# A token-mixing block: the second product over tokens by 2x2 blocks with seven products for eight

## The chip, the cores and the metric

The kernel runs on one core of a Trainium2 chip. A time is the device time of one execution in microseconds; the time of a kernel is the median of its runs. Its engines are TensorE (PE; its weight loads are listed apart as PEld), VectorE (DVE), ScalarE (ACT), GpSimd (POOL) and SyncE (SP), which here issues every DMA. Each engine works through its own queue in order and meets the others at semaphores.

## The reference

One token sequence of S = 2048 tokens with D = 448 channels passes two residual blocks. The second is the one that is changed:

```python
def _B_ref(x, w1, b1, w2, b2):
    h = _layernorm(x, axis=-1)                                  # (B, S, D)
    u = jnp.einsum("bsd,sf->bdf", h, w1) + b1                  # (B, D, F)
    u = _gelu(u)
    y = jnp.einsum("bdf,fs->bds", u, w2) + b2                  # (B, D, S)
    return (lambda x, *d: x.transpose(*d))(y, 0, 2, 1)         # (B, S, D)
...
x = x + ga * _A_ref(h, A_wqkv, A_wo)
h = _layernorm(x, axis=-1) * (1 + cb) + sb
x = x + gb * _B_ref(h, B_w1, B_b1, B_w2, B_b2)
```

The block before it, `_A_ref`, is a linear attention with 16 heads. F is 1792; w1 is 2048 x 1792 and w2 is 1792 x 2048, both in fp32. `mod` rows (`ga`, `cb`, `sb`, `gb` and others) come from a small vector c.

## The kernel before

All of it works on tiles of 128 partitions. Tokens are 16 blocks of 128 (NT), F is 14 blocks of 128 (NF), and the 448 channels are columns. The order of the work is written out by hand: the kernel lists the instructions, and each engine keeps the order of the listing. SBUF tiles come from a pool of 94 slots of 128 x 512 fp32 (`slots`), and a new tile waits until the one that had its slot before is used up. PSUM has 8 banks.

Matmuls of full precision are made of reduced ones. A matrix is split in two F32R tiles, a high part (a rounded copy, ACT) and a low part (the rest, a subtraction on DVE); this is `split`, L52 to L54. A product then takes three matmuls into one PSUM tile: high by high, high by low and low by high (`acc3`, L527 to L530).

The stages are: attention's projections and sums (to about 133 us); attention's output and two layernorms per token block, beside the first four blocks of the first product (to about 240 us); the rest of the first product, u = gelu(h w1), and the second one, y = u w2.

Both products over tokens go through one loop (L624 to L644). w1 and w2 come in pieces of 128 rows and up to 512 columns (`W1G`, `W2G`, `pieces`), loaded 8 steps ahead (`load_to`) and split 3 steps ahead (`split_to`). A step is one piece: for each of its up to four blocks of 128 columns, the three matmuls of `acc3`, with 448 columns of h or u as the moving operand. Each group of blocks has its own PSUM banks, so that the results of the group before are taken out while the next group runs: `finish_u` (L606) makes gelu, the product with gb and the split of one u block, `finish_y` (L614) adds x and stores one block of the output. The residual x waits in 16 slots, and gb * b2 is added to it in the first 16 steps (L640). w2 has six groups, the last two of one block each.

Of the kernel before, what the change touches and what calls it, by code (L numbers as in the profile page):

```python
# [33 lines left out]
def block_kernel(ctx: ExitStack, tc: tile.TileContext, x, wqkv, wo, w1, b1, w2, b2, c, wmod, out):  # L34
    nc = tc.nc
    xf = x.flatten_outer_dims()
    of = out.flatten_outer_dims()

    slots = ctx.enter_context(tc.tile_pool(name="slots", bufs=94))
    small = ctx.enter_context(tc.tile_pool(name="small", bufs=4))  # L40
    cst = ctx.enter_context(tc.tile_pool(name="cst", bufs=1))
    psum = ctx.enter_context(tc.tile_pool(name="psum", bufs=8, space=bass.MemoryType.PSUM))

    ctx.enter_context(tc.manual_schedule())

    def slot(name, w=D, dt=F32, parts=P):
        return slots.tile([parts, w], dt, name=name, tag="slot", padded_shape=[P, 512])

    def bank(name):
        return psum.tile([P, 512], F32, name=name, tag="bank")  # L50

    def split(full, hi, lo):  # L52
        nc.scalar.activation(hi, full, AF.Copy)  # L53
        nc.vector.tensor_sub(lo, full, hi.bitcast(F32))  # L54

# [12 lines left out]
    mhalf = cst.tile([P, 2], F32, name="mhalf")  # L68
    nc.vector.memset(mhalf, -0.5)

# [33 lines left out]
    load_qkv(0)  # L104
    load_x(3)

# [1 line left out]
    warm = bank("warm")  # L108

    def keep_warm(n):  # L110
# [2 lines left out]

    keep_warm(WARM)

# [1 line left out]
    ec = cst.tile([G, 4], F32, name="ec")  # L117
    nc.scalar.activation(ec, c_sb, AF.Exp, scale=-1.0)
    sc = cst.tile([G, 4], F32, name="sc")
# [35 lines left out]
        else:  # L155
            nc.vector.tensor_sub(w[64:128], r[64:128], w[64:128].bitcast(F32))

# [25 lines left out]

# [1 line left out]
    heads, hs, st = {}, {}, {}  # L185

    def a_mean(t):
# [99 lines left out]
    def a_q(t):  # L287
        qps[t] = project(t, 0, "qp")
        del heads[t]
# [61 lines left out]
    for t in range(NT):  # L351
# [42 lines left out]
        if t == 4:  # L394
            for g in range(4):
                w = slot(f"wo{g}", parts=G + 1)
# [3 lines left out]
            b1c = cst.tile([P, NF], F32, name="b1c")  # L400
# [7 lines left out]
            split_to(t + 1 - 16 + PRE)  # L408
    cb1, sb, gb = mods[4], mods[3], mods[5]

# [1 line left out]
    a_q(late.pop(0))  # L412
    load_to(PRE + MID + 3)
    split_to(PRE + MID)
# [10 lines left out]
    nc.scalar.activation(zb, zp[:, :D], AF.Copy)  # L425
    Wph, Wpl = [], []

# [99 lines left out]
    def acc3(ps, hi, lo, sl, mh, ml, first, last):  # L527
        nc.tensor.matmul(ps[:, :D], hi[:, sl], mh, start=first, stop=False)  # L528
        nc.tensor.matmul(ps[:, :D], hi[:, sl], ml, start=False, stop=False)  # L529
        nc.tensor.matmul(ps[:, :D], lo[:, sl], mh, start=False, stop=last)  # L530
# [18 lines left out]
    accs, early = None, []  # L549
    for i in range(NT + LAG):  # L550
# [19 lines left out]
        scale, res, norm1, norm2 = i + 1 < NT, 0 <= i - 2 < NT, 0 <= i - 3 < NT, 0 <= i - 4 < NT  # L570
# [29 lines left out]
        if res or norm1:  # L600
            b_rstd(i, 0 if res else 1, 2 if norm1 else 1)

# [1 line left out]
    Uh, Ul = [None] * NF, [None] * NF  # L604

    def finish_u(f, ps):  # L606
        u = slot(f"u{f}")
        nc.scalar.activation(u, ps[:, :D], AF.Gelu_apprx_tanh, bias=b1c[:, f:f + 1])  # L608
        nc.vector.tensor_mul(u, u, gb)  # L609
        Uh[f] = slot(f"uh{f}", dt=F32R)  # L610
        Ul[f] = slot(f"ul{f}", dt=F32R)
        split(u, Uh[f], Ul[f])

    def finish_y(t, ps):  # L614
        o = slot(f"o{t}")
        nc.vector.tensor_add(o, ps[:, :D], X[t])  # L616
        nc.sync.dma_start(of[t * P:(t + 1) * P, :], o)

    k = NT
    pending = [(finish_u, f, accs[f]) for f in range(4)]  # L620
    xleft = list(range(NT))
    groups = [(w1, f0, n) for f0, n in W1G[1:]] + [(w2, t0, n) for t0, n in W2G]
    k += LAG - 1
    for w, o0, n in groups:  # L624
        up = w is w1
        steps = NT if up else NF
        if early:
            accs, first = early, LAG - 1
            early = None
        else:  # L630
            accs, first = [bank(f"{'up' if up else 'yp'}{o0 + i}") for i in range(n)], 0
        for r in range(first, steps):
            load_to(k + AHEAD)
            split_to(k + 3)
            if pending:
                fn, idx, ps = pending.pop(0)
                fn(idx, ps)
            if xleft:
                t = xleft.pop(0)
                nc.vector.scalar_tensor_tensor(X[t], gb, b2c[:, t:t + 1], X[t], op0=ALU.mult, op1=ALU.add)  # L640
            mh, ml = (H2h[r], H2l[r]) if up else (Uh[r], Ul[r])
            step(k, accs, mh, ml, r == 0, r == steps - 1)
            k += 1
        pending += [(finish_u if up else finish_y, o0 + i, accs[i]) for i in range(n)]  # L644
    for fn, idx, ps in pending:
        fn(idx, ps)


_INS = ['A_x', 'A_wqkv', 'A_wo', 'B_w1', 'B_b1', 'B_w2', 'B_b2', 'c', 'w_mod']
# [23 lines left out]
```

## Time and profile before

| what | value |
|---|---|
| median of 3 runs | 480.47 us (480.19 to 481.48) |
| the profiled execution: span from its first to its last instruction | 476.1 us |
| PE busy | 467.2 us, 98% of the span |
| PEld, DVE, ACT, POOL busy | 425.6, 287.0, 194.2, 26.3 us |
| mean granted TensorE clock | 0.988 |
| first product: first and last matmul start | 159.6 and 335.9 us |
| second product: first and last matmul start | 336.1 and 472.1 us |
| DMA | 45.55 MB, mean 96 GB/s |

The page gives no time for the profiled execution beside its span; the median of the runs is 4.4 us over that span. A group's row has the line of the kernel, the engine, the operation, the tiles that it writes and reads, their shape and number, and then the busy time in us, the mean of one in ns, and the idle time of the engine ahead of them with what ended most of it. A timeline's row has the start and the time from the first to the last end, in us, and the number of instructions that it merges.

### The profile page before, as it was taken

The numbers are of one execution on the slowest core, as the hardware profiler recorded it, in microseconds if no ns is written. First come the engines' busy times: TensorE is split into PE (matmuls) and PEld (weight loads), VectorE is DVE, ScalarE is ACT, GpSimd is POOL, SyncE is SP. The second block draws the span as 40 slices with busy tenths as digits, with TensorE's granted clock in tenths as the row PEclk, the third lists the DMA queues.
The fourth block names the chain that finished last, engine by engine and source line by source line (L and its number), as shares of the span: only waits on it lengthen the run. The fifth ranks groups of instructions, "written<-read, shape, count | busy, mean of one in ns | idle before, by whom it ended". The sixth has DMA issues, their size and how long they took to land.

```text
span 476.1 us, 6824 instructions
## 1 busy us (share of the span) xinstructions
PE 467.2 (98%) x2384; PEld 425.6 (89%) x2384; DVE 287.0 (60%) x672; ACT 194.2 (41%) x419; POOL 26.3 (6%) x62
## 2 busy tenths in 40 slices
PE   6999999999999999999999999999999999999996
PEld 4788899999799999999999999999999999999996
DVE  5789988755888887898538657035620711603243
ACT  1653333335536746666646045034630330500332
POOL 2020211100001010111100000000000000000000
PEclk8799999999999999999999999999999999999999
DMA  8998221005020111112201232018600830801432
GB/s 235 292 274 176 89 67 42 23 23 178 0 67 23 45 44 45 45 45 87 70 1 47 65 111 88 22 53 287 215 0 1 272 115 18 281 0 49 141 115 74
DMA packets 35651, 45.55 MB, mean 96 GB/s; under 512 B 7904, under 2 KB 24096, under 8 KB 35616
## 3 DMA queue, kind: packets, MB, share of 16 engines
q1 hardware_dynamic: 35616, 45.10, 31.5%
q8 instruction: 19, 0.31, 0.3%
q14 instruction: 16, 0.13, 0.1%
HBM read 41.42 MB, written 3.67 MB: 95 GB/s over the span
## 4 chain that ended last, share of the span: by engine, by line
PE 96%; DMA 1%; DVE 1%; SPq 1%; issue 0%; POOL 0%; ACT 0%; DVEq 0%
PE up L530 10%; PE yp L528 10%; PE yp L529 10%; PE up L528 10%; PE yp L530 10%; PE up L529 10%; PE op L477 8%; PE vp L266 8%; PE qp L266 8%; PE kp L266 7%; PE kvb L308 3%; PE tp L247 2%; PE tq L461 1%; DMA wm<-in_w_mod_dram 1%; PE modp L141 1%; PE wp L541 1%
## 5 line engine op out<-in xcount | busy, mean ns | idle before, releaser
L53 ACT ACTIVATE ph<-pr 128x512 fp32r<-128x512 f32 (+2 forms) x148 | 70.1, 518 | 97.3 <-DMA pr<-in_B_w_dram 94.1
L54 DVE TENSOR_TENSOR pl<-pr,ph 128x512 fp32r<-128x512 f32 (+2 forms) x148 | 77.3, 557 | 25.4 <-ACT ph L53 24.5
L530 PE MATMUL up<-h2h,pl 128*128 128x448 f32 x224 | 81.9, 366 | 0.0
L528 PE MATMUL up<-h2h,ph 128*128 128x448 f32 x224 | 81.8, 365 | 0.0
L530 PE MATMUL yp<-uh,pl 128*128 128x448 f32 x224 | 81.8, 365 | 0.0
L528 PE MATMUL yp<-uh,ph 128*128 128x448 f32 x224 | 81.8, 365 | 0.0
L529 PE MATMUL yp<-ul,ph 128*128 128x448 f32 x224 | 81.8, 365 | 0.0
L529 PE MATMUL up<-h2l,ph 128*128 128x448 f32 x224 | 81.8, 365 | 0.0
L616 DVE TENSOR_TENSOR o<-yp,x 128x448 f32<-128x448 f32 x16 | 9.9, 621 | 70.6 <-PE yp L530 70.6
L530 PEld LDWEIGHTS up<-h2h,pl 128*128 128x128 f32 x224 | 42.1, 188 | 3.6 <-DVE pl L54 0.3
L529 PEld LDWEIGHTS up<-h2l,ph 128*128 128x128 f32 x224 | 42.1, 188 | 3.3
L528 PEld LDWEIGHTS up<-h2h,ph 128*128 128x128 f32 x224 | 42.1, 188 | 3.3
L528 PEld LDWEIGHTS yp<-uh,ph 128*128 128x128 f32 x224 | 42.1, 188 | 3.3
L529 PEld LDWEIGHTS yp<-ul,ph 128*128 128x128 f32 x224 | 42.1, 188 | 3.3
L530 PEld LDWEIGHTS yp<-uh,pl 128*128 128x128 f32 x224 | 42.1, 188 | 3.3
L609 DVE TENSOR_TENSOR u<-u,mod 128x448 f32<-128x448 f32 x14 | 8.7, 620 | 40.6 <-ACT u L608 40.6
L608 ACT ACTIVATE u<-up,b1c 128x448 f32<-128x448 f32 x14 | 8.7, 622 | 46.1 <-PE up L530 46.1
L266 PE MATMUL kp<-wh,hh 128*128 128x448 f32 x64 | 24.7, 386 | 0.0
L477 PE MATMUL op<-wph,pth 112*128 112x448 f32 x64 | 24.6, 385 | 0.0
L266 PE MATMUL vp<-wh,hh 128*128 128x448 f32 x64 | 24.6, 384 | 0.0
L266 PE MATMUL qp<-wh,hh 128*128 128x448 f32 x64 | 24.1, 377 | 0.0
L266 PE MATMUL kp<-wh,hl 128*128 128x448 f32 x64 | 23.5, 368 | 0.0
(119 smaller groups left out, 766.2 us busy)
## 6 DMA issues: line engine op xcount, KB each, us to landing
pr<-in_B_w_dram SPq DMA_DIRECT2D x90, 256.0 KB, 3.4
wm<-in_w_mod_dram SPq DMA_DIRECT2D x24, 196.0 KB, 5.7
pr<-in_B_w_dram SPq DMA_DIRECT2D x30, 128.0 KB, 2.4
x<-in_A_x_dram SPq DMA_DIRECT2D x16, 224.0 KB, 4.0
out_dram<-o SPq DMA_DIRECT2D x16, 224.0 KB, 3.1
wr<-in_A_wqkv_dram SPq DMA_DIRECT2D x9, 224.0 KB, 5.3
pr<-in_B_w_dram SPq DMA_DIRECT2D x28, 64.0 KB, 2.0
wo<-in_A_wo_dram SPq DMA_DIRECT2D x4, 196.0 KB, 5.6
```

The source lines that it names most:

```text
L53: nc.scalar.activation(hi, full, AF.Copy)
L54: nc.vector.tensor_sub(lo, full, hi.bitcast(F32))
L247: nc.tensor.transpose(tps[t][:, ch * P:(ch + 1) * P], h[:, ch * P:(ch + 1) * P], ident)
L266: nc.tensor.matmul(o, a[:, s], b, start=(n == 0), stop=(n == 10))
L308: nc.tensor.matmul(kvb[:G + 1, g * G:(g + 1) * G], v[:, g * (G + 1):(g + 1) * (G + 1)], pk[:, g * G:(g + 1) * G], start=(t == 0 and g == 0 ...
L477: nc.tensor.matmul(opb[t][:, :D], a[:, s], b, start=(n == 0), stop=(n == 11))
L528: nc.tensor.matmul(ps[:, :D], hi[:, sl], mh, start=first, stop=False)
L529: nc.tensor.matmul(ps[:, :D], hi[:, sl], ml, start=False, stop=False)
L530: nc.tensor.matmul(ps[:, :D], lo[:, sl], mh, start=False, stop=last)
L608: nc.scalar.activation(u, ps[:, :D], AF.Gelu_apprx_tanh, bias=b1c[:, f:f + 1])
L609: nc.vector.tensor_mul(u, u, gb)
L616: nc.vector.tensor_add(o, ps[:, :D], X[t])
```

## The change

The second product is cut in blocks of 2 x 2: for each pair of token blocks (t0, t1), each pair of f blocks (even and odd), and the two halves of the channels (224 columns each, `HD`). Of such a pair of 2 x 2 matrices the product is formed with seven products of blocks for eight, in the form of Strassen and Winograd. With a11, a12, a21 and a22 for w2's blocks (the first digit of each name goes with the token block, the second with the even or odd f), its sums are s1 = a21 + a22, s2 = s1 - a11, s3 = a11 - a21 and s4 = a12 - s2; u's are t1 to t4, from the halves of an even and an odd u block. The seven products are a11 b11, a12 b21, s2 t2, s1 t1, s3 t3, s4 b22 and a22 t4.

- Each part of u lies in one tile of 448 columns, its high half beside its low half (`u_parts`). A product of two blocks is then two matmuls, the high part of w2 by all 448 columns and the low part by the 224 columns of the high half (`mult2`), and its two column halves are added when it is taken out of PSUM. There are 8 x 7 x 7 = 392 such pairs of matmuls for 672 matmuls of 448 columns.
- w2 is loaded as `a11` to `a22` for all of F and one token block at a time, in tiles of 4 and of 3 blocks, with rows of 512 bytes (`load_quads`). GpSimd makes the sums of w2 (`sums2`, and s4 in `lo2`) and those of u. ACT and DVE split each of the seven operands in high and low parts (`hi2`, `lo2`), two products ahead of PE.
- PSUM tiles are copied (`copy2`) and added to x in place (`out2`, `evac2`), and the output is stored from x.
- x from token block 2 on is written to DRAM in the first product and fetched again a pair at a time (`xpark`, `fetch_x`), and its addition of gb * b2 is made in every second step.
- The first product's third group of four f blocks is cut in two of two.

```diff
-    W1G = [(0, 4), (4, 4), (8, 4), (12, 2)]
-    W2G = [(0, 4), (4, 4), (8, 4), (12, 2), (14, 1), (15, 1)]
+    W1G = [(0, 4), (4, 4), (8, 2), (10, 2), (12, 2)]
     pieces = [(w1, t, f0, n) for f0, n in W1G for t in range(NT)]
-    pieces += [(w2, f, t0, n) for t0, n in W2G for f in range(NF)]
...
+    def u_parts(r, name, src):
+        w = slot(f"u{name}_{r}", dt=F32R)
+        split(src, w[:, :HD], w[:, HD:])
+        uops[name, r] = w
+
+    def finish_u(f, ps):
+        r = f // 2
+
+        def act():
+            u = ufull[f] = slot(f"u{f}")
+            nc.scalar.activation(u, ps[:, :D], AF.Gelu_apprx_tanh, bias=b1c[:, f:f + 1])
+            nc.vector.tensor_mul(u, u, gb)
+            if f % 2 == 0:
+                return
+            u0 = ufull[f - 1]
+            ta, tb = ufull["a", r], ufull["b", r] = slot(f"ta{r}"), slot(f"tb{r}")
+            nc.gpsimd.tensor_tensor(ta[:, :HD], u0[:, HD:], u0[:, :HD], op=ALU.subtract)
+            nc.gpsimd.tensor_tensor(ta[:, HD:], u[:, HD:], ta[:, :HD], op=ALU.subtract)
+            nc.gpsimd.tensor_tensor(tb[:, :HD], u[:, HD:], u0[:, HD:], op=ALU.subtract)
+            nc.gpsimd.tensor_tensor(tb[:, HD:], u[:, :HD], ta[:, HD:], op=ALU.subtract)
+
+        def part(key, half, name):
+            return lambda: u_parts(r, name, ufull[key][:, half * HD:(half + 1) * HD])
+
+        if f % 2 == 0:
+            return [act, part(f, 0, "b11")]
+        two = lambda p, q: lambda: (p(), q())
+        return [act, part(f, 0, "b21"), two(part(("a", r), 1, "t2"), part(("a", r), 0, "t1")),
+                two(part(f, 1, "b22"), part(("b", r), 0, "t3")), part(("b", r), 1, "t4")]
+
+    w2v = w2.rearrange("(r e p) c -> e p r c", e=2, p=P)
...
+    def load_quads(q):
+        for name, (fo, to) in QUADS.items():
+            raw2[q, name] = []
+            for r0, n in RS:
+                w = slot(f"{name}_{q}_{r0}", n * P)
+                c0 = (2 * q + to) * P
+                nc.sync.dma_start(w.rearrange("p (r c) -> p r c", c=P), w2v[fo, :, r0:r0 + n, c0:c0 + P])
+                raw2[q, name].append(w)
+
+    def sub(q, out, a, b, op=ALU.subtract, into=None):
+        res = []
+        for i, (r0, n) in enumerate(RS):
+            w = raw2[q, into][i] if into else slot(f"{out}_{q}_{r0}", n * P)
+            nc.gpsimd.tensor_tensor(w, raw2[q, a][i], raw2[q, b][i], op=op)
+            res.append(w)
+        raw2[q, out] = res
+
+    def sums2(q):
+        sub(q, "s1", "a21", "a22", ALU.add)
+        sub(q, "s2", "s1", "a11")
+        sub(q, "s3", "a11", "a21", into="a21")
+
+    PRODS = (("a11", "b11", 0), ("a12", "b21", 1), ("s2", "t2", 0), ("s1", "t1", 2), ("s3", "t3", 0),
+             ("s4", "b22", 2), ("a22", "t4", 0))
+    todo2 = [(q, m) for q in range(NT // 2) for m in range(7)]
...
+    def hi2(n):
+        while cnt["hi"] < min(n, len(todo2)):
+            q, m = todo2[cnt["hi"]]
+            a = PRODS[m][0]
+            hilo[q, m] = []
+            for w, (r0, nr) in zip(raw2[q, a], RS):
+                h = slot(f"{a}h_{q}_{r0}", nr * P, F32R)
+                nc.scalar.activation(h, w, AF.Copy)
...
+    def lo2(n):
+        while cnt["lo"] < min(n, len(todo2)):
+            q, m = todo2[cnt["lo"]]
+            a = PRODS[m][0]
+            for i, (r0, nr) in enumerate(RS):
+                hl = hilo[q, m][i]
+                hl[1] = slot(f"{a}l_{q}_{r0}", nr * P, F32R)
+                nc.vector.tensor_sub(hl[1], raw2[q, a][i], hl[0].bitcast(F32))
+            cnt["lo"] += 1
+            if a == "a12":
+                sub(q, "s4", "a12", "s2", into="a12")
+
+    def mult2(q, m):
+        a, b, k = PRODS[m]
+        opens = m in (0, 1, 3)
+        if opens:
+            acc2[q, k] = bank(f"y{q}_{k}")
+        ps = acc2[q, k]
+        closes = m in (1, 5, 6)
+        parts2 = hilo.pop((q, m))
+        for r in range(PAIRS):
+            (h, l), i = parts2[r // 4], r % 4
+            w = uops[b, r]
+            s = slice(i * P, (i + 1) * P)
+            nc.tensor.matmul(ps[:, :D], h[:, s], w, start=opens and r == 0, stop=False, skip_group_check=True)
+            nc.tensor.matmul(ps[:, :HD], l[:, s], w[:, :HD], start=False, stop=closes and r == PAIRS - 1,
+                             skip_group_check=True)
+
+    def copy2(q, k, name):
+        cop[q, name] = slot(f"c{name}_{q}")
+        nc.scalar.activation(cop[q, name], acc2[q, k][:, :D], AF.Copy)
+
+    def out2(q, k, name, t, half):
+        c, x = cop.pop((q, name)), X[t][:, half * HD:(half + 1) * HD]
+        nc.vector.tensor_add(c, acc2[q, k][:, :D], c)
+        nc.vector.tensor_add(x, x, c[:, :HD])
+        nc.vector.tensor_add(x, x, c[:, HD:])
...
+    def evac2(q, m):
+        t0, t1 = 2 * q, 2 * q + 1
+        if m == 0:
+            copy2(q, 0, "c1")
+        elif m == 1:
+            out2(q, 1, "c1", t0, 0)
+        elif m == 2:
+            copy2(q, 0, "c2")
+        elif m == 3:
+            copy2(q, 2, "c5")
+        elif m == 4:
+            out2(q, 0, "c5", t1, 1)
+            if q == NT // 2 - 1:
+                store(t1, 1)
+        elif m == 5:
+            out2(q, 2, "c2", t0, 1)
+            store(t0)
+        else:
+            x = X[t1][:, :HD]
+            nc.vector.tensor_add(x, acc2[q, 0][:, :HD], x)
+            nc.vector.tensor_add(x, acc2[q, 0][:, HD:D], x)
+            store(t1, 0 if q == NT // 2 - 1 else None)
...
+    jobs = [j for f in range(4) for j in finish_u(f, accs[f])]
+
+    xleft = list(range(NT))
+    xpark = [park.tile([P, D], F32, name=f"xpark{t}") for t in range(NT)]
+
+    def fetch_x(q):
+        for t in (2 * q, 2 * q + 1):
+            if X[t] is None:
+                X[t] = slot(f"xb{t}")
+                nc.sync.dma_start(X[t], xpark[t])
...
+        for r in range(first, NT):
             load_to(k + AHEAD)
             split_to(k + 3)
+            if jobs:
+                jobs.pop(0)()
+            if xleft and k % 2:
                 t = xleft.pop(0)
                 nc.vector.scalar_tensor_tensor(X[t], gb, b2c[:, t:t + 1], X[t], op0=ALU.mult, op1=ALU.add)
+                if t >= 2:
+                    nc.sync.dma_start(xpark[t], X[t])
+                    X[t] = None
+            step(k, accs, H2h[r], H2l[r], r == 0, r == NT - 1)
             k += 1
+            if k == len(pieces) - 15:
+                load_quads(0)
+            if k == len(pieces) - 12:
+                sums2(0)
+            if len(pieces) - k in (9, 6, 3):
+                hi2(cnt["hi"] + 1)
+                lo2(cnt["lo"] + 1)
+        jobs += [j for i in range(n) for j in finish_u(o0 + i, accs[i])]
+
+    load_quads(1)
+    for i in (0, 2, 1, 3):
+        jobs[i]()
+    jobs = jobs[4:]
+    for n, (q, m) in enumerate(todo2):
+        if m == 0:
+            fetch_x(q)
+        if m == 3 and q + 2 < NT // 2:
+            load_quads(q + 2)
+        hi2(n + 3)
+        lo2(n + 3)
+        if m == 1 and q + 1 < NT // 2:
+            sums2(q + 1)
+        mult2(q, m)
+        if jobs:
+            jobs.pop(0)()
+        evac2(q, m)
...
```

More of the change, by code (lines that the diff above doesn't have):

```diff
@@ L601, in block_kernel @@
             b_rstd(i, 0 if res else 1, 2 if norm1 else 1)
-    Uh, Ul = [None] * NF, [None] * NF
-    def finish_u(f, ps):
[L607 to L617, printed above, removed]
+    HD = D // 2
@@ new lines, in block_kernel @@
+    w2v = w2.rearrange("(r e p) c -> e p r c", e=2, p=P)
+    raw2, comb = {}, {}
+    QUADS = {"a11": (0, 0), "a12": (1, 0), "a21": (0, 1), "a22": (1, 1)}
+    def load_quads(q):
[6 more added lines that the diff above has]
+                raw2[q, name].append(w)
@@ new lines, in block_kernel @@
+    todo2 = [(q, m) for q in range(NT // 2) for m in range(7)]
+    hilo = {}
+    cnt = {"hi": 0, "lo": 0, "quads": 0, "sums": 0}
+    def hi2(n):
[6 more added lines that the diff above has]
+                nc.scalar.activation(h, w, AF.Copy)
+                hilo[q, m].append([h, None])
+            cnt["hi"] += 1
@@ new lines, in copy2, with store @@
+    def copy2(q, k, name):
[6 more added lines that the diff above has]
+        nc.vector.tensor_add(x, x, c[:, HD:])
+    def store(t, half=None):
+        s = slice(0, D) if half is None else slice(half * HD, (half + 1) * HD)
+        nc.sync.dma_start(of[t * P:(t + 1) * P, s], X[t][:, s])
@@ L619, in block_kernel @@
     k = NT
-    pending = [(finish_u, f, accs[f]) for f in range(4)]
+    jobs = [j for f in range(4) for j in finish_u(f, accs[f])]
     xleft = list(range(NT))
-    groups = [(w1, f0, n) for f0, n in W1G[1:]] + [(w2, t0, n) for t0, n in W2G]
+    xpark = [park.tile([P, D], F32, name=f"xpark{t}") for t in range(NT)]
[4 more added lines that the diff above has]
+                nc.sync.dma_start(X[t], xpark[t])
     k += LAG - 1
-    for w, o0, n in groups:
-        up = w is w1
-        steps = NT if up else NF
+    for o0, n in W1G[1:]:
@@ L630, in block_kernel @@
         else:
-            accs, first = [bank(f"{'up' if up else 'yp'}{o0 + i}") for i in range(n)], 0
-        for r in range(first, steps):
+            accs, first = [bank(f"up{o0 + i}") for i in range(n)], 0
+        for r in range(first, NT):
             load_to(k + AHEAD)
             split_to(k + 3)
[L635 to L638, printed above, removed]
+            if jobs:
+                jobs.pop(0)()
+            if xleft and k % 2:
                 t = xleft.pop(0)
                 nc.vector.scalar_tensor_tensor(X[t], gb, b2c[:, t:t + 1], X[t], op0=ALU.mult, op1=ALU.add)
-            mh, ml = (H2h[r], H2l[r]) if up else (Uh[r], Ul[r])
-            step(k, accs, mh, ml, r == 0, r == steps - 1)
+                if t >= 2:
+                    nc.sync.dma_start(xpark[t], X[t])
+                    X[t] = None
+            step(k, accs, H2h[r], H2l[r], r == 0, r == NT - 1)
             k += 1
-        pending += [(finish_u if up else finish_y, o0 + i, accs[i]) for i in range(n)]
-    for fn, idx, ps in pending:
-        fn(idx, ps)
+            if k == len(pieces) - 15:
[23 more added lines that the diff above has]
+        evac2(q, m)
 _INS = ['A_x', 'A_wqkv', 'A_wo', 'B_w1', 'B_b1', 'B_w2', 'B_b2', 'c', 'w_mod']
```

4 lines of the change are left out of this document (added).

## The prediction

> **What bounds the kernel now.** I read the page's first part, then the groups by form, the stage of the second product by a window, and timelines of the spots where one engine holds up another.
>
> ```profile
> span 476.1 us, 6824 instructions
> PE 467.2 (98%) x2384; PEld 425.6 (89%) x2384; DVE 287.0 (60%) x672; ACT 194.2 (41%) x419; POOL 26.3 (6%) x62
> ...
> L530 PE MATMUL yp<-uh,pl 128*128 128x448 f32 x224 | 81.8, 365 | 0.0
> ...
> 335.90:472.40 136.50, 136.50 (x674) 126.18 (x672) 47.43 (x100) 37.51 (x85) 0.00 (x0) 1.00 0.32 104
> ```
>
> The last row is the second product, 335.9 to 472.4 us: PE never stops, the granted clock is 1.00, DVE is busy a third of the time and POOL not at all. 672 matmuls in 136.5 us are 0.203 us each; the 365 ns of a row is latency, since matmuls overlap. So this stage costs matmul starts, and a change pays if it removes starts and nothing else becomes the slowest.
>
> **What a narrower matmul costs.** The new one has 224 columns and no row has that shape with F32R operands. The nearest are at a change from transposes of 128 columns to the projection:
>
> ```profile
> 59.91 0.60 PE L247 MATMUL tp<-ident,h 128*128 128x128 f32 x4
> ...
> 60.23 0.19 PEld L266 LDWEIGHTS vp<-wh,hh 128*128 128x128 f32 x1
> 60.34 0.19 PEld L266 LDWEIGHTS vp<-wl,hh 128*128 128x128 f32 x1
> 60.55 0.19 PEld L266 LDWEIGHTS vp<-wh,hl 128*128 128x128 f32 x1
> ```
>
> Four transposes span 0.60 us with a last one of 0.27, hence 0.11 us from start to start. The F32R weight load at 60.23 is followed by the next after 0.11 us, although each lasts 0.19: loads overlap, and one takes a slot of 0.11. Behind a 448-column matmul the spacing is 0.20 to 0.21. So columns set the 0.203 and the load the 0.11. Half the columns would be 0.203/2 = 0.10, below the load's slot: I take **0.11**. Bounds: 0.109 (the transposes), and 0.203 if the matmul's cost did not fall with its columns.
>
> **The change on PE.** 8 block pairs of tokens x 7 products x 7 pairs of f = 392 pairs of one 448-column and one 224-column matmul, instead of 672 wide ones. 392 x (0.203 + 0.11) = 122.7 us against 136.5: **13.8 us less** if PE stays the bound. One block pair (49 pairs) is then 15.3 us of PE.
>
> **DVE in that stage.** Durations overlap by 0.085 back to back: five pl of 512 columns (686 ns) span 3.09 us, 0.601 each. By the pl rows of 512, 256 and 128 columns (686, 420, 288 ns) and the 621 ns of the 448-column add, less 0.085: 512 is 0.60, 384 is 0.47, 448 is 0.535, 224 is 0.30. Per block pair: the low halves in lo2, 7 x (0.60 + 0.47) = 7.5; the evacuation, 3 x (0.535 + 2 x 0.30) + 2 x 0.30 = 4.0. Sum 11.5 us of 15.3, where before it had 47.4/136.5, one third. ACT: 7 x (0.62 + 0.51) + 3 x 0.54 = 9.5, hidden. The PSUM banks are not reused at once: another product of 2.2 us lies between a copy and the next matmul into its bank.
>
> **POOL in that stage.** It gets s1 to s4 per block pair, 4 x (512 + 384) columns; no such operation is in the trace. Lower bound, the slope of affine_select (677 ns at 448 columns, 292 at 128, so 1.2 ns a column): 0.75 + 0.60, or 5.4 us in all. Upper: POOL's tensor_tensor has a base of 0.41 (0.552 us with one column, 0.691 with two), and two inputs might cost twice the slope: 1.64 + 1.33, 11.9 us. I take base and single slope, 1.02 + 0.87, **7.6 us**, nearer the affine_select, which like the sums has no power in it. [...] Alone, POOL fits too.
>
> **But the two share something.** These rows are, on POOL and DVE, one power that took 0.99 us, and an ordinary one that took 0.55:
>
> ```profile
> 19.18 0.69 DVE L230 SCALAR_TENSOR_TENSOR h<-x,an,mod 128x448 f32<-128x448 f32 x1
> 19.28 0.99 POOL L225 TENSOR_TENSOR rs<-ve,mhalf 128x1 f32<-128x1 f32 x1 [13.28 <-DVE ve L223]
> ...
> 33.84 0.68 DVE L54 TENSOR_TENSOR hl<-tp,hh 128x512 fp32r<-128x512 f32 x1
> 34.07 0.55 POOL L225 TENSOR_TENSOR rs<-ve,mhalf 128x1 f32<-128x1 f32 x1 [4.60 <-DVE ve L223]
> ```
>
> In the first, DVE reads x and mod, both in SBUF, until 19.87, and the power ends 0.40 us after that: it needs whatever DVE holds from 0.14 us after its start. In the second, DVE's tp lies in PSUM, and POOL is not held. Two more powers are stretched the same way (691 ns at 5.3 us, 747 ns at 26.0), and those beside L487, which reads PSUM, are not. So a DVE operation with both inputs in SBUF keeps POOL waiting to its end. All of lo2 and the adds of the copies to x are such: 7.5 + 6 x 0.30 = 9.3 us per block pair. Whether a long POOL operation holds DVE in turn, no row shows.
>
> [...]
>
> If both ways hold, POOL holds 7.6 - 8 x 0.14 = 6.45 us per block pair. DVE plus that is 18.0, or 15.8 if all its 2.2 us on PSUM run under POOL. I take half, 16.9, plus 8 broken overlaps of 0.085: **17.6 us**, over PE's 15.3. DVE's queue then sets the pace, since PE waits for each low half. Before PE can run the last block pair (15.3; POOL has only s4 there), DVE must do 47 of 56 steps of the loop, 6.7 x 17.6 = 117.9, less three low halves made before the stage (3.2), plus the last u pair (0.54 + 7 x 0.30 = 2.6). Stage: 132.6 + 0.3 for the start = 132.9, or **3.6 us less** than 136.5. It breaks even at 18.1 us per block pair.
>
> **The other parts.** At the start of the second product the last u's are late: both gelu, both multiplies and one split lie between the last up matmul and b11 of the last pair, some 2.2 us; it is needed after 6 of 7 steps, 1.9 us. Hence the 0.3; if the chain queued behind the s2 halves it would be 2. The regrouped w1 (two groups of two blocks for one of four) moves no matmul; it adds 16 small loads and splits, and DVE's 0.335 per 256-column split lies in steps of 6 x 0.203 = 1.22 us. The u parts cost DVE 7 x 0.30 instead of 2 x 0.54 per pair, beside PE. POOL's four u sums have 16 steps. Each parked x is a store that waits on SP for its DVE add (L640 before), with the next w1 load queued behind it; loads are 8 steps ahead and splits 3, so 5 steps or 6 us cover a landing of 2.4 to 3.4. Uncovered it would cost about 2 us each. Quads arrive in rows of 512 bytes: the last w2 groups had those too (64 KB, 2.0 us to landing). A block pair moves 1.83 MB of w2, and x in and out, 2.75 MB in 15 us or more, under 185 GB/s, while 289 was reached. fetch_x waits on SP behind the store of the pair before, and DVE needs it about 4.4 us later against a landing of 4.0: covered barely; at worst 1 us per block pair. The tail, two dependent 224-column adds and a half store, is as long as before within 0.2.
>
> **Forecast.** The span is 476.1; the median 480.47 holds 4.4 outside it that I leave. 480.5 - 3.6 = 476.9, less part of a microsecond as POOL often falls into DVE's waits for PE: **476 us**.
>
> **Rivals.**
> - *DVE is never held* (POOL alone waits, in the 15.3 - 9.3 = 6.0 us that DVE leaves, against 6.45): PE keeps the pace, 480.5 - 13.8 + 0.3 + about 1 = 468. For it: no row shows DVE waiting; at 25.47 a power begins and L230 starts 0.18 later with its usual 0.68. [...] 24%.
> - *The two are wholly serial*: no PSUM work falls under POOL, 18.7 us per block pair, stage 6.7 x 18.7 - 0.6 + 15.6 = 140.3, 484 us; at POOL's upper price 22.3 us and 508. It decides from 18.1 on. 22%.
> - *A narrow matmul costs a full slot*: 784 x 0.203 = 159.2, 503 us. It loses from 0.145 on. Against: the loads 0.11 apart. 12%.
> - A late x or a start-up stall adding more than 5 us: 4%.
>
> Forecast itself, 471 to 480: 38%. About 0.3% (1.4 us) is what a measurement can tell from no change. Faster: the 24% and most of the 38%, 0.56; same 0.09; slower 0.35. Range 467 to 492: it leaves out the narrow matmul's 12% and a few per cent of POOL's upper price.
>
> **What would show it.** PE starts in the new stage: 0.203 and 0.11 by pairs where it does not wait. DVE's L693 rows at 686 ns or stretched towards 1.5 us when POOL's L659 runs; L659 itself at about 1.0 and 0.87, or stretched. PE's waits in the stage on DVE's low halves, about 10 us in sum. Wrong would be: L713 spaced like the wide ones, PE without waits, or PE waiting on ACT, DMA or x.

## The result, and the profile after

The changed kernel is slower. Its median is 495.24 us (494.82 to 496.33, 4 runs); the kernel before ran beside it in 480.97 us (4 runs). The ratio is 1.032, with a 95% interval of 1.028 to 1.035. The profiled execution took 494.82 us, with a span of 493.1 us. Every execution of the kernel before that is on record with its span took 1.7 to 1.9 us more than that span. So of the 4.4 us between its median and the span of its profile, some 2.7 are not time outside the span: the profile is of a quicker execution than the median one. On record that kernel took 476.1 to 481.5 us.

These are the span, the busy times and three rows of the forty slices on the page of the changed kernel:

```profile
span 493.1 us, 7571 instructions
PE 464.0 (94%) x2496; PEld 423.4 (86%) x2496; DVE 405.3 (82%) x823; ACT 235.0 (48%) x522; POOL 145.5 (30%) x154
...
PE   6899999999999999999999999979798897897897
DVE  5789988755888878996388598495999999999995
...
POOL 2021110000000110111034242076653954944920
```

PE was full to the end before. Now its row has 7s and 8s in the last third, just where DVE's row goes to 9 and POOL's wakes up. The second product as a window (length; then the busy times of PE, PEld, DVE, ACT and POOL with their instructions; the clock, the DMA share and GB/s), and what PE waited for in the whole execution (total, times, longest):

```profile
341.33:489.26 147.93, 131.48 (x785) 122.80 (x783) 141.81 (x201) 66.90 (x139) 82.56 (x60) 0.95 0.41 123
```

```profile
PE y L713 <- DVE s3l L693: 16.2, 7, 3.6
PE modp L142 <- DVE acc L134: 3.5, 2, 1.9
PE up L529 <- DVE pl L55: 2.9, 2, 2.2
```

DVE, busy a third of this stage before, is now busy 141.81 of 147.93 us. PE stands still seven times, once in every block pair but the last, and each time for the low half of the fifth product (s3l). In the first product it waits twice for a low half of w1 (`pl`), which it did not do before. Why DVE is late is seen in timelines of one block pair, DVE first and POOL after it (start, us, and how many alike in a row):

```profile
399.69 1.15 DVE L693 TENSOR_TENSOR a12l<-a,a12h 128x512 fp32r<-128x512 f32 x2
...
403.76 3.07 DVE L693 TENSOR_TENSOR s1l<-s,s1h 128x512 fp32r<-128x512 f32 x2
406.76 0.61 DVE L722 TENSOR_TENSOR cc<-y,cc 128x448 f32<-128x448 f32 x1
407.40 0.84 DVE L723 TENSOR_TENSOR xb<-xb,cc 128x224 f32<-128x224 f32 x1
408.27 1.07 DVE L724 TENSOR_TENSOR xb<-xb,cc 128x224 f32<-128x224 f32 x1
409.26 3.03 DVE L693 TENSOR_TENSOR s3l<-a,s3h 128x512 fp32r<-128x512 f32 x2
```

```profile
400.51 2.91 POOL L659 TENSOR_TENSOR a<-a,s 128x512 f32<-128x512 f32 x2 [7.14 <-DVE a12l L693]
403.38 3.03 POOL L659 TENSOR_TENSOR s<-a,a 128x512 f32<-128x512 f32 x2
406.38 2.71 POOL L659 TENSOR_TENSOR s<-s,a 128x512 f32<-128x512 f32 x2
409.05 2.82 POOL L659 TENSOR_TENSOR a<-a,a 128x512 f32<-128x512 f32 x2
```

The two halves of a12l (512 and 384 columns), made while POOL rests, take 1.15 us. Those of s1l and s3l, made beside POOL's sums, take 3.07 and 3.03. L723 and L724 are stretched too, from 0.39 to 0.84 and 1.07. L722 between them runs beside a sum as well and keeps its 0.61: one of its inputs, y, lies in PSUM. So in these rows DVE is held by POOL where both its inputs lie in SBUF. POOL is held less: its two sums take 2.9 here, and 1.40 + 1.01 at their fastest.

The 17.0 us by which the span grew (the medians grew by 14.3) are in two places. The second product starts 5.3 us later (336.07 to 341.33), 4.9 of it because the first product is longer. It is itself 11.7 us longer, from its first matmul's start to its last one's end (136.4 to 148.1). The tail differs by less than 0.1.

### The profile page after: what moved, and what is told of

Same layout as the page of the kernel before. It is cut to its first block, busy times and chain, and to the rows that moved or that the text cites. A ratio compares the mean times of both kernels' runs of the same rounds, so it can differ in the third digit from the quotient of the medians.

```text
span 493.1 us, 7571 instructions
## 1 busy us (share of the span) xinstructions
PE 464.0 (94%) x2496; PEld 423.4 (86%) x2496; DVE 405.3 (82%) x823; ACT 235.0 (48%) x522; POOL 145.5 (30%) x154
## 5 line engine op out<-in xcount | busy, mean ns | idle before, releaser
L55 DVE TENSOR_TENSOR pl<-pr,ph 128x256 fp32r<-128x256 f32 (+1 forms) x80 | 46.5, 595 | 10.1 <-ACT ph L54 9.3
L512 POOL TENSOR_TENSOR rt<-vw,mhalf 128x2 f32<-128x2 f32 (+1 forms) x17 | 11.5, 674 | 114.9 <-DVE vw L510 114.9
L718 ACT ACTIVATE cc<-y 128x448 f32<-128x448 f32 x24 | 13.1, 544 | 65.0 <-PE y L713 60.6
L54 ACT ACTIVATE ph<-pr 128x256 fp32r<-128x256 f32 (+1 forms) x80 | 38.3, 492 | 8.9 <-PE up L528 3.9
L659 POOL TENSOR_TENSOR a<-a,s 128x512 f32<-128x512 f32 (+1 forms) x16 | 25.3, 1600 | 56.7 <-DVE a12l L693 56.7
L713 PE MATMUL y<-ut,s3l 128*128 128x224 f32 x56 | 17.4, 311 | 16.2 <-DVE s3l L693 16.2
L713 PEld LDWEIGHTS y<-ut,s3l 128*128 128x128 f32 x56 | 12.4, 221 | 18.4 <-DVE s3l L693 18.2
L626 POOL TENSOR_TENSOR ta<-u 128x224 f32<-128x224 f32 x7 | 10.1, 1437 | 57.8 <-DVE u L621 43.1
L464 ACT ACTIVATE pth<-tq 112x512 fp32r<-112x512 f32 x16 | 9.6, 598 | 33.2 <-PE tq L460 29.4
L265 PE MATMUL kp<-wh,hh 128*128 128x448 f32 x64 | 24.6, 384 | 0.0
L265 PE MATMUL vp<-wh,hh 128*128 128x448 f32 x64 | 24.6, 384 | 0.0
L659 POOL TENSOR_TENSOR s<-a,a 128x512 f32<-128x512 f32 (+1 forms) x16 | 23.7, 1501 | 0.0
```

The costliest lines, as they stand in the source:

```text
L265: nc.tensor.matmul(o, a[:, s], b, start=(n == 0), stop=(n == 10))
L659: nc.gpsimd.tensor_tensor(w, raw2[q, a][i], raw2[q, b][i], op=op)
L713: nc.tensor.matmul(ps[:, :HD], l[:, s], w[:, :HD], start=False, stop=closes and r == PAIRS - 1, skip_group_check=True)
L718: nc.scalar.activation(cop[q, name], acc2[q, k][:, :D], AF.Copy)
```

## The experiments

A time below is a median where several runs were made, and the single run's time otherwise. The kernel before, on the chips of the three sets of runs, had medians of 477.8 (e1 to e4), 478.8 (e5 to e8) and 478.6 us (e9 to e11). "Period" is the time from one block pair's first matmul to the next one's, for a block pair in the middle of the stage. "Stage" is the second product's length as above.

### e1: the sums of w2 on DVE

```diff
-            nc.gpsimd.tensor_tensor(w, raw2[q, a][i], raw2[q, b][i], op=op)
+            nc.vector.tensor_tensor(w, raw2[q, a][i], raw2[q, b][i], op=op)
```

> Edit: the sums of w2 (s1 to s4) on DVE instead of POOL; u's sums stay on POOL. Theory 'port' (a DVE and a POOL operation that both read two SBUF tiles exclude each other): DVE 11.5 + 4 x 1.07 = 15.8 us per block pair against PE's 15.36, nothing is stretched; second product 126 to 132 us instead of 147.9, first product as in the changed kernel, time 473 to 480. Rival 'load' (DVE's own work and its in-order queue, two products ahead, are too much; POOL does not matter): 4.3 us more on DVE per block pair, 18.5 becomes about 22.8, second product about 180, time about 527. Rival 'latency' (POOL's sums are late, DVE waits for them): like 'port', 124 to 130.

477.37 us, ratio 0.998 (0.995 to 1.001): the same time as the kernel before, and 3% less than the changed one. A block pair as a window, and PE's wait:

```profile
372.25:388.92 16.67, 15.63 (x101) 14.66 (x99) 16.43 (x34) 8.37 (x17) 0.00 (x0) 1.00 0.57 166
```

```profile
PE y L713 <- DVE s3l L693: 7.9, 7, 1.8
```

DVE has eight operations more per block pair and is finished earlier: the period falls from a mean of 18.55 us (the second to the seventh block pair) to 16.67. The L693 rows are back at 0.69 and 0.55 us. So the eight sums cost more of DVE's time when POOL makes them than when DVE does. The first product is 177.7 us long instead of 181.2 (176.3 before). The stage takes 134.9 us, more than the 126 to 132 expected by 'port'; 'latency' was given a stage like that of 'port', so this run doesn't tell the two apart.

### e2: no sums of w2

```diff
-        res = []
-        for i, (r0, n) in enumerate(RS):
-            w = raw2[q, into][i] if into else slot(f"{out}_{q}_{r0}", n * P)
-            nc.gpsimd.tensor_tensor(w, raw2[q, a][i], raw2[q, b][i], op=op)
-            res.append(w)
-        raw2[q, out] = res
+        raw2[q, out] = raw2[q, into or a]
```

> Edit: the sums of w2 are left out (the quads themselves are split and multiplied in their place), so POOL is idle in the second product; all splits, matmuls and loads stay. 'Port' and 'latency': PE sets the pace, 8 x 15.36 = 123 us plus under 2 at the start, time about 472. 'Load': second product stays at 147.9, time 495.

464.15 us. This is the second product as a window:

```profile
335.08:458.46 123.38, 123.08 (x785) 117.29 (x783) 100.78 (x201) 65.54 (x139) 3.16 (x4) 1.00 0.49 145
```

PE never stops for more than 0.4 us, the period is 15.35 us, and the first product is back at 176.3. What the changed kernel loses against this, 24.6 us in the second product and 4.9 in the first, hangs on the sums of w2. The time is 8 us under the 472 expected: 4.9 are the first product, where no gain was reckoned with, and the kernel before is 3 us quicker on this chip too.

### e3: POOL only writes

```diff
-            nc.gpsimd.tensor_tensor(w, raw2[q, a][i], raw2[q, b][i], op=op)
+            for _ in range(3):
+                nc.gpsimd.memset(w, 0.5)
```

> Edit: each sum of w2 becomes three memsets of the same tile on POOL: POOL is occupied for about as long (512 columns took 1.40 us, a memset of 448 took 0.47), the tiles and the waits on them stay, the values of the sums are left out. POOL then reads nothing. 'Port' (only reads collide): L693 back at 0.68 and 0.55 us, second product 123 to 127, time about 472 to 476. 'Latency': stalls at s3 as before, 140 to 148, time about 490 to 495. 'Load': 147.9, 495.

464.67 us. One block pair:

```profile
366.90:382.20 15.30, 15.30 (x100) 14.62 (x99) 12.42 (x26) 8.16 (x17) 10.94 (x24) 1.00 0.63 181
```

POOL is as busy as in the changed kernel (10.94 us of a period, 11.4 there), and DVE's rows are not stretched: it needs 12.42 us. So neither the time that POOL is busy nor the waits between the two queues hold DVE, but that POOL reads from SBUF: DVE is busy 12.42 us of a block pair beside writes, and in the changed kernel 18.3 beside reads (the mean of the last two windows of this document). The stage of 123.5 us is the one that 'port' expected; the time is below its 472 to 476, for the same reasons as in e2.

### e4: the sums of u on DVE

The four `nc.gpsimd.tensor_tensor` of `finish_u` become `nc.vector.tensor_tensor`; the sums of w2 stay on POOL.

> Edit: the four sums of each u pair on DVE instead of POOL; w2's sums stay on POOL. 'Port': the last up matmul, 5.2 us later than in the kernel before, comes within 2 us of it, since pl and ub splits are no longer held; second product about 148 as in the changed kernel; time 490 to 492. 'Load': DVE gets 1.2 us more per u pair, the last up matmul is 5 to 9 us late, time 495 to 499.

494.28 us, 1.034 of the kernel before beside it: no better than the changed kernel. The first product is 179.5 us long, so at most 1.7 of its 4.9 us more come from the sums of u; the rest is from the first sums of w2 (e2). Both expectations missed: the last `up` matmul is 3.2 us later than in the kernel before (expected were within 2, or 5 to 9), and the time lies between the two ranges. PE's waits in the stage are as they were:

```profile
PE y L713 <- DVE s3l L693: 15.7, 7, 2.9
```

### e5: the sums on DVE, spread over the block pair

From e1, with s3 at the block pair's own first product and s1 and s2 of the next one at its third and fourth, instead of all three at the second:

```diff
-        if m == 1 and q + 1 < NT // 2:
-            sums2(q + 1)
+        if m == 0:
+            sums2(q, 3)
+        if m in (2, 3) and q + 1 < NT // 2:
+            sums2(q + 1, m - 1)
```

> Edit: w2's sums on DVE as in the first experiment, but spread: s1 and s2 of the next block pair at the third and fourth product of this one, s3 at its own first product, instead of six operations in a row (3.2 us) that left PE waiting 1.3 us per block pair. Theory 'clump': DVE's 15.8 us per block pair against PE's 15.36 leave 0.4, stage 126 to 129 instead of 134.9, time 5 to 8 us below the first experiment and 1.0 to 1.8% below the kernel before. Rival 'sum': DVE's total is already more than it can do beside its waits, the 1.3 us per block pair stay wherever the sums stand, same time as the first experiment.

474.82 us, ratio 0.992 (0.989 to 0.995): 0.8% faster than the kernel before. PE's wait has moved to another operation and is shorter, but there is one in each block pair still:

```profile
PE y L718 <- DVE cc L728: 6.5, 7, 1.0
```

The period is 16.67 us to the hundredth, as in e1. Where the sums stand does not matter for it; their total does. The spread pays only at the start: 176.3 us for the first product and 17.3 instead of 19.6 for the first block pair. The stage is 133.0 us, so the 126 to 129 of 'clump' missed; 'sum' had the period right.

### e6: half the sums on POOL

From e5, with s3 and s4 on POOL.

> Edit: the spread order, s1 and s2 on DVE, s3 and s4 on POOL. 'Port', a price per POOL operation: DVE lost 6.8 us per block pair to eight POOL operations, so 3.4 to four; 11.5 + 2.1 + 3.4 = 17.0 us per block pair, stage about 136, time 8 to 10 us above the spread sums on DVE. Rival 'burst': only eight in a row outlast the two products that DVE is ahead, four (two and two apart) are absorbed: stage 124 to 128, time as with the spread sums on DVE or below.

481.96 us, stage 140.7. One block pair:

```profile
406.82:424.46 17.64, 15.93 (x101) 14.67 (x99) 17.40 (x30) 8.50 (x17) 5.97 (x4) 1.00 0.54 157
```

The three periods lie on one line with DVE's own work, 12.4 us (e3). Eight sums on DVE make it 16.67, so 0.535 each. Eight on POOL make it 18.55, so 0.77 each. Half and half it should be 12.4 + 4 x 0.535 + 4 x 0.77 = 17.6, and it is 17.64. The expected 17.0 and 136 were too low, since they took DVE's own work at 11.5.

### e7: the kernel before, with idle work on POOL

In the second product of the kernel before, POOL gets 26 subtractions whose result nobody uses, and then 42 memsets of the same tile:

```diff
+            if not up and o0 < 8 and (o0 or r > 1):
+                nc.gpsimd.tensor_tensor(mods[2], Uh[NF - 1].bitcast(F32), mods[1], op=ALU.subtract)
+            elif not up and o0 == 8:
+                for _ in range(3):
+                    nc.gpsimd.memset(mods[2], 0.5)
```

> Edit to the kernel before, nothing of the change in it: 26 subtractions of 128 x 448 columns, both inputs in SBUF, queued on POOL from the first group of the second product on, and 42 memsets of 128 x 448 behind them; their result is not used. 'Port': the pl subtractions (686 ns) beside the POOL subtractions take 1.0 to 1.5 us, beside the memsets 0.69; the adds of L616, which read PSUM, stay at 0.62. PE does not wait, since DVE has two thirds of the stage free: time within 1.5 us of the kernel before. Rival (the stretch belongs to the tiles that POOL and DVE share, not to the port): pl stays at 0.69 throughout.

479.41 us. Here the price stands by itself, without one queue waiting for the other. The groups of POOL, and DVE's splits in a stretch beside each of them (350 to 362 and 378 to 398 us):

```profile
L644 POOL TENSOR_TENSOR mod<-uh,mod 128x448 f32<-128x448 f32 x26 | 36.4, 1399 | 105.2 <-ACT uh L53 103.2
L647 POOL MEMSET mod<- 128x448 f32 x42 | 19.9, 473 | 2.4
```

```profile
L54 DVE TENSOR_TENSOR pl<-pr,ph 128x512 fp32r<-128x512 f32 x7 | 11.0, 1637 | 0.0
```

```profile
L54 DVE TENSOR_TENSOR pl<-pr,ph 128x512 fp32r<-128x512 f32 x8 | 5.3, 690 | 1.3 <-ACT ph L53 1.2
```

1.64 us beside subtractions, 0.69 beside memsets. And the two take turns, one operation each, as these two rows of timelines show:

```profile
348.91 10.99 DVE L54 TENSOR_TENSOR pl<-pr,ph 128x512 fp32r<-128x512 f32 x7
```

```profile
350.07 12.07 POOL L644 TENSOR_TENSOR mod<-uh,mod 128x448 f32<-128x448 f32 x8
```

Seven splits in 10.99 us and eight subtractions in 12.07: less the last of each (1.64 and 1.15, the latter with no split beside it), 1.56 us from start to start for both. The fastest subtraction took 1.15 (1.23 from start to start), and DVE's operation 0.60 from start to start, 1.75 to 1.83 together. So they run almost one after the other, with 0.2 to 0.3 us shared. The stretch is over the upper end of the expected 1.0 to 1.5 us; four adds of L616, which read PSUM, run beside the subtractions and keep their 0.62. PE did not wait, since DVE has room in the kernel before. Its starts are 0.207 us apart in this execution and 0.203 in the profile of the kernel before; whether POOL's work has a part in that, the runs do not show.

### e8: operands three products ahead

```diff
-        hi2(n + 3)
-        lo2(n + 3)
+        hi2(n + 4)
+        lo2(n + 4)
```

> Edit to the changed kernel: the halves are split three products ahead instead of two; sums stay on POOL. 'Port': DVE with its stretch needs 18.3 us per block pair however early it may start, so the stage loses at most 2 to 4 us of 147.9, time 491 to 495. Rival 'short queue': the burst of POOL is absorbed by the longer lead, 126 to 132, time 475 to 480.

490.11 us. A block pair as a window:

```profile
414.62:432.78 18.16, 16.27 (x100) 14.65 (x99) 17.92 (x26) 8.40 (x17) 11.00 (x9) 1.00 0.50 153
```

What PE waited for has changed:

```profile
PE y L712 <- ACT cc L718: 8.8, 6, 2.3
```

That copy stands in ACT's queue behind a high half (a22h), which waits up to 4.3 us for an add of DVE. So the chain goes through ACT, and DVE still gives the pace. The period falls by 0.4 us only, to 18.16, of which DVE works 17.92; the rest is about the gap of 0.03 to 0.04 us ahead of each of its seven dependent adds (e10). A longer lead can't help where DVE's total is the limit. That a short queue ahead of PE was the cause falls. By e6's reckoning a sum on POOL costs DVE 0.72 us here, so the 0.77 is no constant.

### e9: three narrow matmuls

From e5. The wide matmul is cut in two that add into the same 224 columns, so that the two column halves need not be added by DVE:

```diff
-            nc.tensor.matmul(ps[:, :D], h[:, s], w, start=opens and r == 0, stop=False, skip_group_check=True)
+            nc.tensor.matmul(ps[:, :HD], h[:, s], w[:, :HD], start=opens and r == 0, stop=False, skip_group_check=True)
+            nc.tensor.matmul(ps[:, :HD], h[:, s], w[:, HD:], start=False, stop=False, skip_group_check=True)
...
-        nc.vector.tensor_add(c, acc2[q, k][:, :D], c)
+        nc.vector.tensor_add(c[:, :HD], acc2[q, k][:, :HD], c[:, :HD])
...
-        nc.vector.tensor_add(x, x, c[:, HD:])
```

> The spread version on DVE (e5), with the 448-column matmul of each pair replaced by two of 224 columns (high half by high, high half by low) that add into the same 224 columns of the bank. PE then has 8 x 7 x 7 x 3 = 1176 starts of 224 columns; the copies and the adds of the evacuation are half as wide, and four of the seven adds of low columns are gone. DVE's work per block pair falls by 3 x (0.535 - 0.30) + 4 x 0.39 = 2.3 us, from 16.67 to about 14.4. Theory 1 (DVE's queue is what holds PE in e5, and a narrow start is 0.101 us as in the changed kernel): the pace is PE's 147 x 0.101 = 14.85 us per block pair, the stage 8 x 14.85 + 1 = 120, the time 474.8 - 13 = 462. Theory 2 (a 224-column start that must bring its own weight load each time takes the load's 0.109): 16.0 us per block pair, stage 129, 471. Rival (the pace is set by a wait chain between the two engines and not by DVE's sum): 16.67 stays, 475.

473.23 us, ratio 0.989 (0.986 to 0.992). PE does not wait for anything in the stage:

```profile
401.40:417.80 16.40, 16.40 (x149) 16.40 (x149) 14.68 (x30) 7.60 (x17) 0.00 (x0) 1.00 0.57 169
```

DVE fell to 14.7 us (14.4 was reckoned), and PE became the limit: 16.41 us for 147 starts is 0.112 each. That is theory 2, a shade worse than its 16.0. Where a narrow matmul follows a wide one in the changed kernel, its start is 0.101 us from the next; behind another narrow one it is 0.112. But the wide one ahead of it takes 0.213 there, and 0.203 to 0.207 among its like, so nothing shows that the narrow one as such is cheaper in a pair. The work taken from DVE was put on PE.

### e10: the dependent adds between the low halves

From e5. The two adds of a product to x, each of which needs the result of the one before it, are put in a list, and each low half takes one from there:

```diff
                 nc.vector.tensor_sub(hl[1], raw2[q, a][i], hl[0].bitcast(F32))
+                if pend:
+                    pend.pop(0)()
...
-        nc.vector.tensor_add(x, x, c[:, :HD])
-        nc.vector.tensor_add(x, x, c[:, HD:])
+        pend.append(lambda: nc.vector.tensor_add(x, x, c[:, :HD]))
+        pend.append(lambda: nc.vector.tensor_add(x, x, c[:, HD:]))
```

> The spread version on DVE (e5), with the adds of a product's evacuation no longer back to back: the add of the bank comes first, and each dependent add follows one of the next low halves. Theory (DVE's sum sets the pace, and a dependent add costs 0.43 us instead of 0.30 because it waits for the end of the one before it): 7 such adds per block pair give back 7 x 0.13 = 0.9 us, 15.75 for 16.67, still over PE's 15.36; the stage is 132.8 - 6 = 126.5 and the time about 468 to 469. Rival (the 0.13 us is the operation's own, or the adds delay the low halves that PE waits for by as much): 16.67 stays, 474.8.

470.43 us, ratio 0.981 (0.977 to 0.985): the fastest version of all, 1.9% under the kernel before. The same adds in timelines, first of e5, then of e10:

```profile
415.23 0.62 DVE L728 TENSOR_TENSOR cc<-y,cc 128x448 f32<-128x448 f32 x1
415.88 0.39 DVE L729 TENSOR_TENSOR xb<-xb,cc 128x224 f32<-128x224 f32 x1
416.31 0.39 DVE L730 TENSOR_TENSOR xb<-xb,cc 128x224 f32<-128x224 f32 x1
416.61 1.15 DVE L699 TENSOR_TENSOR a11l<-a,a11h 128x512 fp32r<-128x512 f32 x2
```

```profile
414.07 0.62 DVE L735 TENSOR_TENSOR cc<-y,cc 128x448 f32<-128x448 f32 x1
414.60 0.68 DVE L704 TENSOR_TENSOR a11l<-a,a11h 128x512 fp32r<-128x512 f32 x1
415.20 0.39 DVE L736 TENSOR_TENSOR xb<-xb,cc 128x224 f32<-128x224 f32 x1
415.50 0.55 DVE L704 TENSOR_TENSOR a11l<-a,a11h 128x384 fp32r<-128x384 f32 x1
```

By starts: from L728 to the add that needs it 0.65 us, and 0.43 from there to the next dependent one; then 0.30 to the low half, which needs neither. In e10 the same add of the bank is followed after 0.53, and an add to x after 0.30. The durations in the rows are alike; only the starts tell it. Seven such places at about 0.13 us are 0.9, and the period fell by that, from 16.67 to 15.79, with DVE busy all of it:

```profile
417.09:432.88 15.79, 15.59 (x101) 14.66 (x99) 15.79 (x34) 8.28 (x17) 0.00 (x0) 1.00 0.62 175
```

### e11: both edits

> Both edits on the spread version: three narrow matmuls per pair and the adds between the low halves. DVE falls to about 14 us per block pair. By theory 1 of the narrow matmuls PE sets the pace at 14.85 us and the time is that of the narrow version alone, 462; by theory 2 at 16.0, 471, again that of the narrow version alone. If the narrow version is still held by DVE, this one is faster than it by up to 0.4 us per block pair, 3 us in all.

472.50 us, ratio 0.987 (0.984 to 0.990), with a period of 16.41 us for 147 starts, again 0.112 each; DVE is busy 14.4 us of it. The narrow version is held by PE, so DVE's saving buys nothing there.

## Why the prediction was wrong

Forecast were 476 us and a range of 467 to 492; it is 495.2. The mechanism was named, POOL's hold on DVE as an assumption: a DVE operation with both inputs in SBUF and a reading POOL operation keep each other out (in e7 0.69 us of DVE became 1.64, and 1.15 of POOL 1.48), DVE's queue then sets the pace, and PE waits for low halves. The signs it asked for came: rows of L693 stretched toward 1.5 us and beyond, PE's waits on low halves. PE's wait in the stage was put at about 10 us and was 16.2. What failed are terms of the sum: the span was to fall by 4.5 us and grew by 17.0, and of the 21.5 us between, 15.2 lie in the second product (its formula, with DVE's own work in it) and 4.9 in the first, which was put at nothing.

**What held.** The matmul pair was put at 0.203 + 0.11 us, 15.3 per block pair; it takes 0.213 + 0.101 = 0.314, 15.35, and e2's stage is 123.5 us beside the forecast 122.7. In the stage PE never waited for a parked x, for the quads or for another DMA. The tail is as long as it was.

**DVE's own work, 11.5 us per block pair.** It is 12.4 (e3). The evacuation was costed with the overlap of 0.085 us between neighbours, but its adds depend on each other: 0.65 + 0.43 + 0.30 for an evacuated product instead of 0.535 + 2 x 0.30, and 0.72 instead of 0.60 for the last. That is 3 x 0.25 + 0.12 = 0.9, and e10 took it back by order alone.

**POOL's sums, 7.6 us per block pair.** The four sums were put at 1.02 and 0.87 us for 512 and 384 columns. The fastest of each took 1.40 (perhaps not free of DVE) and 1.01, 9.6 for the four sums, and a burst in place takes 11.4. My bounds of 5.4 to 11.9 held it; the value taken from affine_select's slope was too low.

**What POOL costs DVE, 17.6 - 11.5 = 6.1 us.** Measured 18.55 - 12.4 = 6.15. That POOL holds DVE at all no row of the kernel before shows, so the term was an assumption of mine; e7 shows the hold, 1.64 us for 0.69, and no run shows the half that was taken between 15.8 and 18.0. The size was right by luck, since two errors cancel: POOL's work is longer than I had it, and it holds DVE for a smaller share of it, 0.77 us for each sum, whose mean is 1.2 us at its fastest and 1.4 in place.

**The stage's formula, 6.7 x 17.6 - 3.2 + 2.6 + 15.6 = 132.9.** It is 148.1. The last low half that PE waits for is ready 127.3 us after the stage's start where the formula has 117.3, and what PE has left after it takes 20.8 us and not 15.6. Of the 10.0, DVE's longer own work is an estimated 5.7 (0.9 in 6.3 block pairs). DVE also idled 3.8 us up to 467.5 us, 1.8 of it until PE had finished products, for which the formula had nothing; the smaller differences the runs do not separate. The 5.2 come from where the sums stand: I spread their price evenly over a block pair, and it all falls into the first five products. So PE stops last at the fifth product of the seventh block pair, with nearly ten products to go, and the formula lets it run through the last seven. It need not be POOL: in e1, with the sums on DVE in the same place, PE's last long stop is at the same product, and in e5, where they are spread, two products later with 17.9 us to go. The break-even was put at 18.1 us per block pair; e6 with 17.64 has a stage of 140.7 us and e5 with 16.67 one of 133.0, so by an estimate between them it lies near 17.1.

**The first product, at nothing.** It is 4.9 us longer. "POOL's four u sums have 16 steps" and "DVE's 0.335 per 256-column split lies in steps of 6 x 0.203 = 1.22 us" looked at each by itself, and did not apply the exclusion taken for the next stage to this one. The first sums of w2 are queued on POOL here, beside DVE's splits of w1. POOL's and DVE's timelines:

```profile
322.31 2.67 POOL L659 TENSOR_TENSOR s<-a,a 128x512 f32<-128x512 f32 x2
324.94 2.58 POOL L659 TENSOR_TENSOR s<-s,a 128x512 f32<-128x512 f32 x2
```

```profile
322.27 0.43 DVE L55 TENSOR_TENSOR pl<-pr,ph 128x256 fp32r<-128x256 f32 x1 [0.45 <-ACT ph L54]
322.61 2.61 DVE L55 TENSOR_TENSOR ut<-ta,ut 128x224 fp32r<-128x224 f32 x2
325.14 1.50 DVE L55 TENSOR_TENSOR pl<-pr,ph 128x256 fp32r<-128x256 f32 x1
```

A split of 256 columns takes 0.43 us ahead of the sums and 1.50 beside them, and two of 224 columns 2.61. Three operations take 4 us, so the lead of three steps (3.7 us) is gone. PE's two waits for `pl` make 2.9 us, and behind the longer one ten matmuls start 0.35 to 0.37 us apart instead of 0.20, 1.7 more. That it is the sums is shown by e2 and e5, both at 176.3 us.

**The rivals.** That DVE is never held (24%) falls by e7: 1.64 for 0.69 us. That the two are wholly serial (22%) had nearly the right period, 18.7, but L722 did run beside a sum; by the same formula its stage is too short, 140.3, and its 484 is 11 us off, for that reason and for the first product. A narrow matmul at a full slot (12%) falls: 0.101, and 0.112 among its like. A start-up stall of over 5 us (4%) did not come: the second product starts 0.2 us behind the last start of the first, as before. The 4.9 us are lost ahead of it.

The chance of 0.56 for faster rested on gaining 3.6 us out of 13.8, with the terms that had bounds taken at or below their middle. Apart from the price of POOL, where two errors cancelled, the errors named above all went the same way.

## What to carry to other kernels

An add moved from DVE to POOL to relieve DVE can cost DVE more than keeping it: here 0.77 us for 0.535, in a stage where the low halves, which read two SBUF tiles, are 7.5 (7 x 1.07 from start to start) of DVE's own 12.4 us. Before such a move, count what share of the busy engine's work has two SBUF inputs, in every stage in which the moved work is queued, and price the move by that. And when an engine is the limit, look at the starts and not at the durations of its rows: putting independent work between dependent adds gave 0.9 us of a period of 16.7, with no operation removed.

## What the runs showed of the hardware that I had not expected

- The two do not share the loss evenly: in e7 POOL's subtraction went from 1.15 at its fastest to 1.48 us beside the splits, and DVE's split from 0.69 to 1.64.
- DVE's next operation started 0.085 us before the one ahead of it ended (`pl` rows of 0.686 us, 0.601 from start to start, in the kernel before), but a dependent one 0.03 to 0.04 after it (e5's rows under e10).
- A wide and a narrow matmul together took 0.314 us, close to 0.203 + 0.11; the 0.101 of the narrow one's own start could not be had without the wide one, since narrow ones among themselves took 0.112.
- In the changed kernel's second product, pauses of 2.02 to 2.04 us between starts of PE left the clock alone (1.00 in their block pairs), and after pauses of 2.31 to 3.93 us, at once or some four pairs later, five or six matmul pairs started 0.59 us apart instead of 0.31, at a clock of 0.50 (354.6 to 357.7 us). In e1 the same followed one of 2.21 us (0.91 from 336.2 to 355.8 us). Block pairs of 17.3 and 20.1 us alternate in the changed kernel, and the slower clock (0.92) falls in the long ones:

```profile
381.80:399.10 17.30, 15.65 (x101) 14.66 (x100) 17.08 (x24) 8.39 (x17) 11.39 (x8) 1.00 0.54 161
399.10:419.20 20.10, 17.25 (x101) 16.08 (x100) 19.55 (x29) 8.40 (x17) 11.37 (x8) 0.92 0.47 137
```

Whether the slower clock brings about the alternation, and whether it costs time by itself here, where DVE sets the pace, was not tried. In e8 the pauses from the third block pair on are 1.8 us at most, the clock stays at 1.00 and nothing alternates, with a period of 18.16 us where these two have a mean of 18.7.
